# Taking a decay factor from a float32 exponential by DMA from chunk 8 on instead of chunk 12, in a fused linear-attention and feed-forward kernel

## The chip, the cores and the metric

The kernel runs on one core of a Trainium2 chip. The metric is the device time of one execution in microseconds (us). A core has a matrix engine (TensorE, PE in the profile, with its weight loads as PEld), a vector engine (VectorE, DVE), a scalar engine (ScalarE, ACT), a third elementwise engine (GpSimd, POOL) and SyncE (SP), which here issues all DMAs. Each engine works through its own list of instructions in order and waits on semaphores for the others.

## The reference, cut to what matters

The inputs are `q`, `k`, `v` and `alpha`, each of 4 batches x 8 heads x 768 positions x 48 (alpha between 0.8 and 1), and two weight matrices. First a gated linear attention:

```
state = alpha[t][:, None] * state + outer(k[t], v[t])    # 48 x 48 per batch and head
y[t]  = q[t] @ state
```

Then the heads are put side by side (3072 tokens x 384) and go through a feed-forward layer: `h = x @ w_in` (384 to 2048), `g = max(h, 0) ** 2`, `out = g @ w_out` (2048 to 384). All is float32 outside; the kernel computes its matmuls in bfloat16.

## The kernel before, in words

**Chunks.** The 3072 tokens are 24 chunks of 128 positions, 6 to a batch, and the recurrence is rewritten for chunks. With L = log(alpha) and the prefix sum of L inside the chunk, A = exp(prefix sum) and Ai = exp(-prefix sum) are factors per position, and qA = q * A, kI = k * Ai. Inside a chunk y is the masked score matrix (qA times kI transposed, positions up to the own one) times v; what came before adds qA times the running state. At the end of a chunk the state becomes (state + kI transposed times v) * ae, where ae = exp(sum of L over the whole chunk), one number for each of the 48 key dimensions of each head. So ae is equal to the last row (position 127) of A. The first four chunks are done as two pairs by another function (`add_super`, lines 593 to 775); chunks 4 to 23 by `add_chunk`, `add_scores` and `add_back`.

**The steps of a chunk** and their lines:

- four loads of 192 KB (alpha, q, k, v), issued by SP (line 349), up to six chunks ahead, in tiles that hold two chunks; the next user of a tile waits for the readers of the one before
- the logarithm of alpha into `L_s` on ScalarE (line 407), the cast of v to bfloat16 on GpSimd (line 412)
- `e_p0`, on TensorE: the prefix sum, one matmul of 128x384 with the triangle `utri_b` (line 417); in chunks under `TURN` four more matmuls of one column each (`L_s` as the weights, `ones_col` as the moving operand, line 419), which leave the chunk's sum with the key dimensions on the partitions
- on ScalarE: A (`e_A`, line 435) and Ai (`e_Ai`, line 439). In chunks under `TURN`, A is bfloat16, and two small exponentials (lines 442 and 445) turn the sums into `ae_s`. From `TURN` on, A is float32 (the tile `Af`, in which the element order is permuted so that the four head pairs of one key dimension lie side by side), and SP moves its last row into `ae_s` with two DMAs of 48 partitions x 4 values (`e_aed`, line 452)
- on VectorE: `qA_s` (line 463, or 466 when A is float32) and `kI_s` (line 469); both are transposed on TensorE (line 258 through a helper) and copied out by VectorE (`qkT`, line 372)
- scores on TensorE for two chunks at once from chunk 8 on (`e_p2`, into the tile `sc` and two further banks), masked by VectorE (`sm`, line 530)
- `e_ps` (line 555): kI transposed times v is added to the state in PSUM; this operation waits for `kI_s`, the cast v, `ae_s` and the copy of the state of the chunk before. `e_stm` on VectorE (line 564) multiplies the state by ae, `e_sb` on ScalarE (line 569) copies it out in bfloat16 for the next chunk. The last chunk of a batch has none of these three, but its factor is still written
- the output `e_p3a`, `e_p3b`, a copy (`xn`, line 370), a transpose and a copy into `xT_big`

Feed-forward work runs in groups of one, two or four chunks: the first layer (`add_moe1`: matmuls of `xT_big` with `w_in_b`), relu on ScalarE (line 819), square on VectorE (line 827), the second layer (`add_moe2`: 16 matmuls of 128x384 a chunk), a copy out of PSUM (lines 889, 891) and a store issued by SP (lines 898, 901).

**Order.** Nothing of this order is left to the chip. Each operation is put into a plan with its engine, an assumed duration, its predecessors and a priority; `Plan.run` (lines 99 to 143) places all of them by these numbers and the instructions are then written out in that order, engine by engine. The assumed durations are constants in the code, among them those that depend on `TURN`: a load 1.05 or 0.97, the prefix sum 0.27 or 0.17, A 0.38 or 0.76, `qA_s` 0.47 or 0.78, and for the factor's DMAs 0.4 plus a latency `AE_LAT` of 4.0, during which the planner puts other work before `e_ps`. A gate lets the prefix sum of a chunk start only when the feed-forward work has come far enough. PSUM has eight banks; five are shared by all of these steps, and a step takes a bank when its reader has released it.

Of the kernel before, what the change touches and what calls it, by code (L numbers as in the profile page):

```python
# [146 lines left out]
def kernel(  # L147
# [86 lines left out]
    w_out_b = consts.tile([P, FT, d_model], BF16)  # L234

    NBUF = 4
    TURN = 12
    AE_LAT = 4.0
    L_s = big.tile([P, NBUF, H, DP], BF16)
    nc.gpsimd.memset(L_s[:, :, :, D:], 0.0)  # L240
# [13 lines left out]
    def mm(*a, **kw):  # L254
        pin(nc.tensor.matmul(*a, **kw))  # L255
# [23 lines left out]
    def add(eng, dur, emit, *deps, **kw):  # L279
        return plan.add(Op(eng, dur, emit, deps, **kw))  # L280
# [59 lines left out]
    def add_load(s, nm):  # L340
# [10 lines left out]
        if 2 * NS <= s < 2 * NS + LB and (k - LB // 2) < NS:  # L351
            prev = SUP[k - LB // 2]["use_" + nm]
        pace = C[s - LB + 1]["use_" + nm] if s >= TURN + 2 else None
        d["ld_" + nm] = add("DMA", LD if s < TURN else 0.97, ld, prev, pace, lat=2.4)

# [41 lines left out]
    def add_chunk(s):  # L397
# [17 lines left out]
        def e_p0():  # L415
            pm = d["pm"] = psum(p0, [P, 512], FP32)
            mm(pm[:, 0:HD], lhsT=utri_b[:, 0, :], rhs=L[:, :, 0:D], start=True, stop=True)
            for p in range(NP if s < TURN else 0):
                mm(pm[:, HD + p:HD + p + 1], lhsT=L[:, 2 * p:2 * p + 2, :], rhs=ones_col,
                   start=True, stop=True)  # L420
        p0 = Op("PE", 0.27 if s < TURN else 0.17, e_p0, [ln], takes=GLA_BANKS, lat=0.17, **g)
        p0.gla = s

        def split(x, s):
            if s < TURN:
                return x.rearrange("p (h d) -> p h d", h=H)
            return x.rearrange("p (n j d) -> p n j d", n=NP, j=2)

        def e_A():
            if s < TURN:  # L430
                d["A"] = work.tile([P, H, D], BF16, name="A")
            else:
                d["Af"] = work.tile([P, 2, D, NP], FP32, name="Af", bufs=2)
                d["A"] = d["Af"].rearrange("p j d n -> p n j d")
            pin(nc.scalar.activation(d["A"], split(d["pm"][:, 0:HD], s), AF.Exp))  # L435
# [566 lines left out]
```

## Time and profile before

| what | value |
|---|---|
| median of 3 runs | 186.08 us (185.95 to 186.28) |
| the profiled execution | 185.27 us, of which its span is 183.6 us |
| granted TensorE clock | 1.00 throughout |
| ScalarE, A in bfloat16 (line 435, 8 times) | 491 ns |
| ScalarE, A in float32 (line 435, 12 times) | 867 ns |
| ScalarE, lines 442 and 445 (8 times each) | 168 ns |
| VectorE, `qA_s` from A (line 463, 8 times) | 580 ns |
| VectorE, `qA_s` from Af (line 466, 12 times) | 859 ns |
| SP, loads of chunks 4 to 23 (80 of 192 KB) | 3.6 to 3.7 us to landing |
| SP, `ae_s` from Af (line 452, 24 of 0.8 KB) | 2.0 us to landing |

How to read it: the span runs from the first to the last instruction of the profiled execution, and the time of the execution is a little longer. A row of a group gives the engine, the line, what is written and read, how often, and the mean duration; a line can be that of a helper (255 and 258 for TensorE's matmuls and transposes). The mean duration of a matmul includes its run through the engine; consecutive matmuls overlap, and what one costs is read from the distance of the starts. The chain is the work that ended last, followed back from its end; what is not on it ran beside it. "To landing" is from the issue on SP to the arrival of the data.

### The profile page before, as it was taken

The numbers are of one execution on the slowest core, as the hardware profiler recorded it, in microseconds if no ns is written. First come the engines' busy times: TensorE is split into PE (matmuls) and PEld (weight loads), VectorE is DVE, ScalarE is ACT, GpSimd is POOL, SyncE is SP. The second block draws the span as 40 slices with busy tenths as digits, with TensorE's granted clock in tenths as the row PEclk, the third lists the DMA queues.
The fourth block names the chain that finished last, engine by engine and source line by source line (L and its number), as shares of the span: only waits on it lengthen the run. The fifth ranks groups of instructions, "written<-read, shape, count | busy, mean of one in ns | idle before, by whom it ended". The sixth has DMA issues, their size and how long they took to land.

```text
span 183.6 us, 5043 instructions
## 1 busy us (share of the span) xinstructions
PE 177.2 (97%) x2000; PEld 133.5 (73%) x2000; DVE 135.0 (74%) x282; ACT 121.6 (66%) x257; POOL 30.5 (17%) x48
## 2 busy tenths in 40 slices
PE   7889899999999999999999999999999999999994
PEld 2567684666987877878867877777877878767863
DVE  6688779576998797776884997966996988852600
ACT  2567789357996994767739857847848768633721
POOL 6044667612111111111011011010010000000000
DMA  6999999899997989895999796877701101012012
GB/s 147 261 279 321 319 361 366 167 224 227 162 221 148 207 171 217 187 210 123 202 230 217 176 212 157 182 143 163 186 0 43 47 2 47 2 43 89 0 43 88
DMA packets 101256, 30.23 MB, mean 165 GB/s; under 512 B 93680, under 2 KB 100464, under 8 KB 101232
## 3 DMA queue, kind: packets, MB, share of 16 engines
q1 hardware_dynamic: 101232, 29.91, 70.2%
q8 instruction: 15, 0.25, 0.6%
q14 instruction: 9, 0.07, 0.1%
HBM read 25.17 MB, written 4.72 MB: 163 GB/s over the span
## 4 chain that ended last, share of the span: by engine, by line
PE 85%; ACT 5%; DMA 3%; DVE 3%; SPq 2%; issue 1%; ACTq 0%
PE bank L255 74%; PE bank L258 7%; DMA at<-in_alpha_dram 3%; PE sc L255 2%; PE st L255 2%; SPq L365 2%; ACT r L819 1%; DVE sm L530 1%; DVE qkT L372 1%; ACT raw L717 1%; ACT L_s L605 0%; DVE qA_s L653 0%; ACT w_in_b L308 0%; DVE st L747 0%; ACT L_s L407 0%
## 5 line engine op out<-in xcount | busy, mean ns | idle before, releaser
L255 PE MATMUL bank<-xT_big,w_in_b 128*128 128x256 bf16 (+2 forms) x600 | 73.3, 268 | 0.0
L255 PE MATMUL bank<-w_out_b,gT 128*128 128x384 bf16 (+2 forms) x400 | 71.9, 319 | 0.0
L819 ACT ACTIVATE r<-bank 128x512 bf16<-128x512 f32 x96 | 56.2, 603 | 15.6 <-PE bank L255 13.6
L255 PEld LDWEIGHTS <-w_in_b 128*128 128x128 bf16 x600 | 53.1, 98 | 9.4
L827 DVE TENSOR_TENSOR gT<-r 128x512 bf16<-128x512 bf16 x96 | 43.9, 480 | 11.5 <-ACT r L819 10.8
L255 PEld LDWEIGHTS <-gT 128*128 128x128 bf16 x400 | 36.3, 98 | 17.6
L412 POOL CAST vb<-vt 128x384 bf16<-128x384 f32 x20 | 11.0, 552 | 91.2 <-PE bank L255 56.7
L372 DVE COPY qkT<-bank 128x1024 bf16<-128x1024 bf16 (+1 forms) x26 | 16.4, 645 | 3.6 <-PE bank L258 3.4
L891 ACT COPY ob<-bank 128x384 f32<-128x384 f32 x17 | 8.2, 480 | 13.9 <-PE bank L255 13.7
L370 ACT CAST xn<-bank 128x384 bf16<-128x384 f32 x24 | 11.3, 483 | 9.0 <-PE bank L255 8.8
L530 DVE TENSOR_TENSOR sm<-sc,utri_b 128x512 bf16<-128x512 f32 x24 | 15.4, 683 | 2.0 <-PE sc L255 1.9
L372 DVE COPY xT_big<-bank 128x384 bf16<-128x384 bf16 x21 | 7.4, 354 | 10.8 <-PE bank L258 10.8
L255 PEld LDWEIGHTS <-qkT 64*128 64x128 bf16 (+2 forms) x304 | 10.5, 97 | 5.4 <-issue 2.2
L466 DVE TENSOR_TENSOR qA_s<-qt,Af 128x384 bf16<-128x384 f32 x12 | 10.3, 859 | 2.7 <-ACT Af L435 2.7
L407 ACT ACTIVATE L_s<-at 128x384 bf16<-128x384 f32 x20 | 10.4, 525 | 2.5 <-DMA at<-in_alpha_dram 2.5
L435 ACT ACTIVATE Af<-bank 128x384 f32<-128x384 f32 x12 | 10.4, 867 | 1.6 <-ACT xn L370 1.0
L469 DVE TENSOR_TENSOR kI_s<-kt,Ainv 128x384 bf16<-128x384 f32 x20 | 11.0, 552 | 0.0
L569 ACT CAST sb<-st 128x384 bf16<-128x384 f32 x16 | 7.7, 482 | 4.4 <-DVE st L564 4.3
L439 ACT ACTIVATE Ainv<-bank 128x384 bf16<-128x384 f32 x20 | 10.3, 513 | 0.0
L530 DVE TENSOR_TENSOR sm<-bank,utri_b 128x512 bf16<-128x512 f32 x16 | 10.2, 680 | 0.0
L255 PE MATMUL bank<-warm 128*128 128x256 bf16 (+2 forms) x36 | 8.1, 357 | 1.9 <-DVE both L218 1.1
L258 PE MATMUL bank<-ident_bf,qA_s 128*128 128x128 bf16 x96 | 9.3, 219 | 0.5 <-DVE qA_s L653 0.3
(73 smaller groups left out, 177.3 us busy)
## 6 DMA issues: line engine op xcount, KB each, us to landing
at<-in_alpha_dram SPq DMA_DIRECT2D x20, 192.0 KB, 3.6
qt<-in_q_dram SPq DMA_DIRECT2D x20, 192.0 KB, 3.7
kt<-in_k_dram SPq DMA_DIRECT2D x20, 192.0 KB, 3.7
vt<-in_v_dram SPq DMA_DIRECT2D x20, 192.0 KB, 3.7
out_dram<-ob SPq DMA_DIRECT2D x19, 192.0 KB, 2.7
wo<-in_moe_w_out_dram SPq DMA_DIRECT2D x4, 768.0 KB, 7.4
wi<-in_moe_w_in_dram SPq DMA_DIRECT2D x4, 384.0 KB, 7.2
wi<-in_moe_w_in_dram SPq DMA_DIRECT2D x2, 768.0 KB, 5.7
```

Of the source, the lines that this page charges most:

```text
L255: pin(nc.tensor.matmul(*a, **kw))
L258: pin(nc.tensor.transpose(*a))
L370: pin(nc.scalar.copy(out_t, in_t))
L372: pin(nc.vector.tensor_copy(out_t, in_t))
L407: pin(nc.scalar.activation(L[:, :, 0:D], d["at"], AF.Ln))
L412: pin(nc.gpsimd.tensor_copy(d["vb"], d["vt"]))
L435: pin(nc.scalar.activation(d["A"], split(d["pm"][:, 0:HD], s), AF.Exp))
L439: pin(nc.scalar.activation(d["Ai"], d["pm"][:, 0:HD].rearrange("p (h d) -> p h d", h=H), AF.Exp, scale=-1.0))
L469: pin(nc.vector.tensor_mul(kI[:, :, 0:D], d["kt"], d["Ai"]))
L530: pin(nc.vector.tensor_mul(d["sm"][:, hh], d["sc"][hh], utri_b.to_broadcast([P, NP, P])))
L819: pin(nc.scalar.activation(box["r"][:, 0:w], box["ph"][:, 0:w], AF.Relu))
L827: pin(nc.vector.tensor_mul(gT[g][:, f0:f0 + per, lo * P:lo * P + n], r, r))
```

## The change

`TURN` goes from 12 to 8. Chunks 8, 9, 10 and 11 now take their decay factor as chunks 12 to 23 do: their prefix sum has no `ones_col` matmuls, A is written as `Af` in float32, the two small exponentials are gone, `qA_s` is computed from `Af`, and two DMAs bring the factor into `ae_s`. The planner's constants for these four chunks change with it, and so does the pace that it assumes for the loads of chunks 10 to 13 (line 353), so that it places the work of these and the following chunks in another order. Up to the prefix sum of chunk 8 the order of TensorE's instructions is the one before.

```
     NBUF = 4
-    TURN = 12
+    TURN = 8
     AE_LAT = 4.0
```

The lines that read it:

```
pace = C[s - LB + 1]["use_" + nm] if s >= TURN + 2 else None
d["ld_" + nm] = add("DMA", LD if s < TURN else 0.97, ld, prev, pace, lat=2.4)
...
for p in range(NP if s < TURN else 0):
...
a_ = add("ACT", 0.38 if s < TURN else 0.76, e_A, p0, **g)
...
if s < TURN:
    ae0 = add("ACT", 0.18, e_ae0, p0, after(ai), **g)
    p0.gives = ae1 = add("ACT", 0.19, e_ae1, p0, after(ae0), **g)
else:
    p0.gives = ai
    ae1 = add("SPD", 0.4, e_aed, a_, lat=AE_LAT, **g)
    ae1.hold = 0.5
```

In SP's list the new pairs of DMAs stand: chunk 8's between the loads of chunk 9 and those of chunk 10; chunk 9's between those of chunk 10 and those of chunk 11; chunk 10's after the alpha and q loads of chunk 13; chunk 11's after the alpha load of chunk 14.

## The prediction

> **What bounds the kernel now.** I read the engine totals first, then the chain that ended last, then the busy times by stage, and last the places where the changed instructions stand. The totals and the chain by line of the page of before:
>
> ```profile
> span 183.6 us, 5043 instructions
> PE 177.2 (97%) x2000; PEld 133.5 (73%) x2000; DVE 135.0 (74%) x282; ACT 121.6 (66%) x257; POOL 30.5 (17%) x48
> PE 85%; ACT 5%; DMA 3%; DVE 3%; SPq 2%; issue 1%; ACTq 0%
> ```
>
> TensorE is busy for 97% and carries 85% of the chain. A pipelined busy time can hide waits, so I also read the chain in order of time (start, length, what). This stretch is the only one after 24 us in which the chain leaves TensorE for long:
>
> ```profile
> 58.27 0.66 PE bank L255 x4
> 58.95 0.26 ACT ob L891
> ...
> 61.24 0.17 ACT ae_s L445
> ...
> 63.82 1.89 DVE sm L530 x3
> 65.76 2.47 PE bank L255 x37
> ...
> 166.43 14.39 PE bank L255 x120
> 180.85 0.27 ACT ob L855
> ```
>
> From 58.95 to 65.76 us the chain runs through ScalarE and VectorE, but TensorE is not idle for it: in this stretch the timeline shows one real hole, where the last matmul of one group starts at 65.43 us and the next at 65.76, 0.33 where this form (three 128x256 matmuls in 0.33 us elsewhere in the chain) takes 0.11: 0.22 us lost. From 65.76 to 180.85 nothing but TensorE is on the chain. So after 24 us the time is the sum of what TensorE issues, plus whatever holds it.
>
> The stages (busy us per engine, granted clock, DMA share, GB/s), with the change inside the second and third:
>
> ```profile
> 54.00:66.00 12.00, 11.94 (x153) 9.67 (x151) 10.18 (x22) 9.63 (x25) 1.01 (x2) 1.00 0.88 172
> 66.00:82.00 16.00, 16.00 (x192) 12.37 (x189) 12.78 (x29) 10.85 (x26) 2.32 (x4) 1.00 1.00 205
> 82.00:166.00 84.00, 84.00 (x912) 64.85 (x910) 66.39 (x135) 57.40 (x113) 4.70 (x9) 1.00 0.53 123
> ```
>
> VectorE has 1.8 us free of 12, then 3.2 of 16. The DMA engines, at 0.53 where the present factor DMAs run, are full where the new ones go.
>
> **The change part by part.** For chunks 8 to 11 each:
>
> (1) TensorE drops the four `ones_col` matmuls of 128x1. The price is read from starts of neighbours in the timeline, first chunk 9, then chunk 12:
>
> ```profile
> 58.76 0.33 PE L255 MATMUL bank<-L_s,utri_b 128*128 128x384 bf16 x1
> 58.92 0.24 PE L255 MATMUL bank<-ones_col,L_s 128*128 128x1 bf16 x4
> 59.02 0.38 PE L255 MATMUL bank<-xT_big,w_in_b 128*128 128x256 bf16 x2
> ...
> 81.73 0.33 PE L255 MATMUL bank<-L_s,utri_b 128*128 128x384 bf16 x1
> 81.89 0.49 PE L255 MATMUL bank<-w_out_b,gT 128*128 128x384 bf16 x2
> ```
>
> With them the next matmul starts 59.02 - 58.76 = 0.26 us after the prefix-sum matmul, without them 81.89 - 81.73 = 0.16: 0.10 to 0.105 per chunk, 4 x 0.105 = 0.42 us, all on the path. The weight loads of these four (96 ns mean of the 48 loads from `L_s`) would be 16 x 0.096 = 1.5 us if they stood on the path; 0.105 for four of them says that they hide under the 128x384 matmul. The Trainium skill, "TensorE: Matmul & The Clock Gate", section "LDWEIGHTS (loading the stationary operand)", gives a load as its columns over 1.2, 107 ns for 128, an estimated 16 x 0.107 = 1.7 us if it bound here; by that rule the sum would be -1.7 instead of -0.42, and the trace speaks against it.
>
> (2) ScalarE: the first exponential writes float32 in a strided layout (Af, 867 ns mean of 12) instead of bfloat16 (A, 491 ns), +0.376; the two exponentials into `ae_s` (0.168 each, 0.336) go. Sum +0.04 per chunk, +0.16 in all. VectorE: `qA_s` from Af takes 859 ns, from A 580: +0.28, +1.1 us in all. Neither engine sets the pace in the present Af stage (57.4 and 66.4 of 84 us), so I cost them at nothing. What hides them is the matmuls in between; if that cover is gone the +1.1 is the upper bound, and below it is zero, since both engines gain work.
>
> (3) SP and DMA: per chunk two transfers of 0.8 KB, eight in all, in the same queue as the loads. The rows:
>
> ```profile
> L452 SPq DMA_DIRECT2D ae_s<-Af x24: 501/583/1281, 83.0 to 156.8; - x24
> DMA to landing us min/median/max: 1.6/2.0/3.3
> ```
>
> Two issues take about 1.2 us of SP (0.58 each). In the new order the pair of chunk 8 stands between the loads of chunks 9 and 10, that of chunk 9 between those of 10 and 11, that of chunk 10 behind the alpha and q loads of chunk 13, and that of chunk 11 behind alpha of chunk 14 (nothing reads that one, chunk 11 closes a batch). So every load behind them goes out up to 1.2 us later per pair, less where SP was held by a full queue anyway (at chunk 9's v load for 2.63 us, at chunk 12's alpha load for 2.02). The loads that ScalarE needs soonest are alpha of 11, 12 and 13: the 11th was issued at 59.22, the group of them landed in 3.4 to 4.4 us (median 3.8), and its logarithm started at 64.98. That leaves about 2 us for it. For 12 and 13 (issued 63.35 and 67.72, logarithms at 68.84 and 73.03) it leaves 1.7 and 1.5 before their two pairs' delay of at most 2.4. A logarithm that is 0.5 us late holds the relu behind it on ScalarE, and so a bank of TensorE. I take nothing, with 0 to 0.5 us as bounds.
>
> (4) The new wait: the state matmul (`e_ps`, line 560) now waits for the landing. TensorE runs in a fixed order, so everything behind it would wait too. The planner moves the state matmuls of chunks 8, 9 and 10 back behind other matmuls, so I compare times. State matmul of chunk 8: from the prefix-sum matmul of chunk 8 at 54.22, the new order has two prefix-sum matmuls (0.32), 9 first-layer matmuls of 128 columns (0.50), 16 of 384 columns (2.60), 11 transposes (0.61), the output group (0.37) and 15 of 256 columns (1.65): 6.05, so it stands at 60.3. In the same way chunk 9's stands at about 64.5 and chunk 10's at about 75.0. Landings: Af of chunk 8 would be ready at 54.73 + 0.87 = 55.6, SP is free at 55.66, the second issue starts at about 56.3 and lands at 58.3 (median) to 59.6 (longest). Chunk 9: second issue at about 61.0, landing 63.0 to 64.3. Chunk 10: second issue between 70.7 and 72.6, landing 72.7 to 75.9. At the median all three are in time, by 2.0, 1.5 and 0.4 to 2.3 us. I cost this wait at nothing, as the rows of this very transfer lie nearest. Its other end: a load at this place took up to 4.9 us (v, issues from 49.7 to 70.5); with that the lateness would be 0.9, 1.4 and up to 2.5 us, and since an earlier hold moves the later ones back, 2.5 us in all.
>
> The 0.22 us hole at 65.43 waits for VectorE's mask of the scores, behind a square that came late. The new order has another square there, so it may close; I count 0 to 0.22 as gain and take 0.
>
> Sum on the profiled execution: 183.6 - 0.42 = 183.2 us of span. That execution took 185.27, so 1.67 lies around its span; 184.85. It was 0.81 under the median of the runs shown, 186.08. Carried over: 186.08 - 0.42 = 185.66.
>
> **The rivals.**
>
> A. A late factor. As in (4): one landing that passes the 4.0 us that chunk 8 has, or the 3.5 that chunk 9 has, holds TensorE. For it: DMA share 0.88 to 1.00 here against 0.53 in the later stage, and the loads' 3.4 to 4.9 us. Against it: the small transfer has 0.8 KB where a load has 192, and 3.3 us was the longest of 24. It decides from 0.42 us of lateness on, that is 4.4 us for chunk 8 or 3.9 for chunk 9. One miss of 0.9: 186.08 - 0.42 + 0.9 = 186.6; all of it: 188.2. The Trainium skill, "DMA: Bandwidth & Descriptors", section "Anatomy of one DMA — SWDGE (gpsimd) path", puts a constant of about 2.0 us on every DMA; by that figure no landing is late and the sum stays at -0.42. The trace's 1.6 to 3.3 us is not constant, and the rows decide.
>
> B. VectorE becomes the bound. It is 85% busy from 54 to 66 us, and the chain already ran through it. All of (2) on the path: 186.08 - 0.42 + 1.1 + 0.16 = 186.9. Against it: from 82 us on the same forms run with TensorE at 84.0 of 84.0.
>
> C. The gain is eaten in part: a late logarithm or mask holds a bank for 0.2 to 0.4 us. 185.9.
>
> D. The 16 dropped weight loads were on the path after all, at 0.096 each: 186.08 - 1.5 = 184.6. Only the difference of the two starts in (1) speaks for or against it, and it is against.
>
> **How the numbers follow.** Forecast (185.66) 0.50; C 0.20; A 0.21; B 0.07; D 0.02. About 0.2%, 0.37 us, is what a measurement of this kernel can tell from no change. Faster: forecast and D, 0.52. Within: C, 0.20. Slower: A and B, 0.28. The range goes from 185.2 (the forecast less the hole of 0.22 and the runs' scatter of 0.2) to 187.0 (over B and a single miss in A); outside lie D and the worse half of A. The likeliest case by itself: 185.2 to 185.8.
>
> **What the changed profile would show.** (1) 16 `ones_col` matmuls instead of 32, and 0.16 us from prefix sum to next matmul at chunks 8 to 11. (2) 16 instructions each of Af and of `qA_s` from Af, 4 left in each `ae_s` line of ScalarE. (3) 32 issues at line 452, the first at about 56 us. (4) The state matmuls of chunks 8, 9, 10 at about 60.3, 64.5 and 75.0 with no hole before them. What would make me wrong: a hole before one of these with the `ae_s` DMA as its releaser (A), chain pieces of line 466 and 530 with holes after them (B), or a logarithm at line 407 that waits for its DMA (C).

## The result

The changed kernel is slower. Its median is 187.49 us (185.53 to 188.24, 18 runs) against 185.87 us (185.30 to 187.51, 18 runs) for the kernel before on the same chip: a ratio of 1.0082, with a 95% interval of 1.006 to 1.0103. The forecast was 185.66, with a range up to 187.0; both missed, and on the wrong side of no change. The profiled execution took 186.64 us with a span of 184.9, 1.3 more than the 183.6 before; it is one of the quicker ones of its kernel, so it shows most of the loss but not all of it.

### The profile page after: what moved, and what is told of

Read it like the earlier page. It is cut to its first block, busy times and chain, and to the rows that moved or that the text cites. A ratio compares the mean times of both kernels' runs of the same rounds, so it can differ in the third digit from the quotient of the medians.

```text
span 184.9 us, 5017 instructions
## 1 busy us (share of the span) xinstructions
PE 177.8 (96%) x1983; PEld 133.0 (72%) x1984; DVE 137.1 (74%) x284; ACT 121.2 (66%) x247; POOL 29.9 (16%) x48
## 4 chain that ended last, share of the span: by engine, by line
PE 80%; DMA 5%; ACT 5%; SPq 4%; DVE 3%; issue 1%; ACTq 0%
PE bank L255 69%; PE bank L258 7%; DMA at<-in_alpha_dram 5%; SPq L349 2%; PE sc L255 2%; SPq L365 2%; PE st L255 2%; ACT r L819 1%; DVE sm L530 1%; DVE qkT L372 1%; ACT Af L435 1%; ACT raw L717 1%; DVE qA_s L466 0%; ACT L_s L605 0%; DVE qA_s L653 0%
## 5 line engine op out<-in xcount | busy, mean ns | idle before, releaser
L891 ACT COPY ob<-bank 128x384 f32<-128x384 f32 x15 | 7.3, 484 | 15.9 <-PE bank L255 15.8
L466 DVE TENSOR_TENSOR qA_s<-qt,Af 128x384 bf16<-128x384 f32 x16 | 13.7, 859 | 5.3 <-ACT Af L435 5.3
L435 ACT ACTIVATE Af<-bank 128x384 f32<-128x384 f32 x16 | 13.9, 866 | 1.7 <-ACT xn L370 1.0
L564 DVE TENSOR_TENSOR st<-st,ae_s 128x384 f32<-128x384 f32 x16 | 9.0, 560 | 2.1 <-PE bank L255 1.3
```

What stands on the lines that cost most here:

```text
L466: pin(nc.vector.tensor_mul(qA[:, :, 0:D].rearrange(v4, j=2), d["qt"].rearrange(v4, j=2), d["A"]))
```

## The profile after

The totals and the chain by engine on the page of the changed kernel:

```profile
span 184.9 us, 5017 instructions
...
PE 177.8 (96%) x1983; PEld 133.0 (72%) x1984; DVE 137.1 (74%) x284; ACT 121.2 (66%) x247; POOL 29.9 (16%) x48
...
PE 80%; DMA 5%; ACT 5%; SPq 4%; DVE 3%; issue 1%; ACTq 0%
```

TensorE's share of the chain fell from 85 to 80%; SP's queue doubled to 4% and DMA rose from 3 to 5%. After 24 us the chain, in order of time (start, length, what), now leaves TensorE for long at two places:

```profile
60.81 0.58 SPq L452
61.40 0.05 issue
61.45 0.58 SPq L349
...
63.34 2.58 SPq L349
...
65.96 3.40 DMA at<-in_alpha_dram
...
69.81 0.85 ACT Af L435
...
70.68 0.87 DVE qA_s L466
...
105.92 1.10 ACT r L819 x2
...
107.04 0.42 DVE gT L827
107.46 1.81 DVE sm L530 x3
...
109.32 1.55 PE bank L255 x28
```

The first place runs, after some work of ScalarE, through one of the new factor issues (line 452). Behind it stand the four loads of a chunk, behind them the alpha load of the next (issued at 65.96), and behind its landing the logarithm and the exponential on ScalarE and `qA_s` on VectorE. The second place, at 106 us, lies 30 us behind the four chunks that were changed. By stage (busy us per engine, granted clock, DMA share, GB/s):

```profile
54.00:66.00 12.00, 12.00 (x141) 9.62 (x136) 10.63 (x23) 9.01 (x19) 1.49 (x3) 1.00 0.79 153
66.00:82.00 16.00, 15.89 (x163) 11.60 (x161) 13.16 (x28) 10.32 (x20) 1.54 (x3) 1.00 0.88 175
...
100.00:124.00 24.00, 23.23 (x254) 17.64 (x252) 19.88 (x40) 15.47 (x30) 1.82 (x3) 1.00 0.84 181
```

From 54 to 82 us the DMA engines moved less than before (153 and 175 GB/s against 172 and 205) although they had more to do. So the loss is not a want of DMA engines; the loads are issued late. And TensorE, at 24.00 of 24.00 from 100 to 124 us before, lost 0.77 us there.

Two rows of the groups say who waits. The last part of a row is the idle time of the engine ahead of the group, and what ended it. First before, then after:

```profile
L407 ACT ACTIVATE L_s<-at 128x384 bf16<-128x384 f32 x20 | 10.4, 525 | 2.5 <-DMA at<-in_alpha_dram 2.5
L564 DVE TENSOR_TENSOR st<-st,ae_s 128x384 f32<-128x384 f32 x16 | 8.9, 556 | 0.0
```

```profile
L407 ACT ACTIVATE L_s<-at 128x384 bf16<-128x384 f32 x20 | 10.3, 528 | 6.1 <-DMA at<-in_alpha_dram 6.1
L564 DVE TENSOR_TENSOR st<-st,ae_s 128x384 f32<-128x384 f32 x16 | 9.0, 560 | 2.1 <-PE bank L255 1.3 <-PE bank L258 0.8
```

ScalarE waits 3.6 us more for alpha: the logarithms of chunks 11, 12 and 13 waited 1.49, 0.79 and 1.00 us, where before none of them waited more than 0.03. VectorE, which before never waited ahead of the state multiply (`e_stm`, line 564), now waits 2.1 us. The row names TensorE as the releaser, but TensorE was long done. VectorE's timeline around the multiply of chunk 14, before and after (start, length, then the instruction):

```profile
102.88 1.09 DVE L827 TENSOR_TENSOR gT<-r 128x512 bf16<-128x512 bf16 x3
103.88 0.56 DVE L564 TENSOR_TENSOR st<-st,ae_s 128x384 f32<-128x384 f32 x1
104.35 0.68 DVE L372 COPY qkT<-bank 128x1024 bf16<-128x1024 bf16 x1
```

```profile
103.27 0.55 DVE L469 TENSOR_TENSOR kI_s<-kt,Ainv 128x384 bf16<-128x384 f32 x1
104.94 0.57 DVE L564 TENSOR_TENSOR st<-st,ae_s 128x384 f32<-128x384 f32 x1 [1.12 <-PE bank L255]
105.41 0.42 DVE L827 TENSOR_TENSOR gT<-r 128x512 bf16<-128x512 bf16 x1
105.75 0.68 DVE L372 COPY qkT<-bank 128x1024 bf16<-128x1024 bf16 x1
```

The state matmuls of chunk 14 (`e_ps`) had run from 102.85 on, without waiting for the factor: only the multiply reads `ae_s`. The second factor transfer landed at 104.82, and the multiply began 0.12 us later, as it did at the other two late chunks (90.41 and 90.54; 119.01 and 119.13). So it waited for the factor. Behind it in VectorE's list stand a square and the copy `qkT`, and TensorE waits for that copy, then for the masks:

```profile
106.49 0.40 PE L255 MATMUL bank<-qkT 64*128 64x128 bf16 x8 [0.57 <-DVE qkT L372]
...
109.32 0.33 PE L255 MATMUL bank<-sb,qkT 128*128 128x96 bf16 x4 [0.20 <-DVE sm L530]
```

Measured by the distance of the starts, these two holes are about 0.75 and 0.36 us. The waits at chunks 12 and 16 (0.21 and 0.78 us) left none of this size in this execution. The cause is seen in SP's list, before and after:

```profile
99.43 0.73 SPq L898 DMA_DIRECT2D out_dram<-ob  x1
100.22 0.42 SPq L349 DMA_DIRECT2D at<-in_alpha_dram  x1
100.74 1.29 SPq L452 DMA_DIRECT2D ae_s<-Af  x2
```

```profile
97.89 0.43 SPq L349 DMA_DIRECT2D at<-in_alpha_dram  x1
98.43 2.35 SPq L349 DMA_DIRECT2D qt<-in_q_dram  x1
100.87 1.20 SPq L349 DMA_DIRECT2D kt<-in_k_dram  x1
102.16 1.21 SPq L452 DMA_DIRECT2D ae_s<-Af  x2
```

`Af` of chunk 14 was ready at 97.81 (before: 98.70), yet its two factor DMAs were issued at 102.16 (before: 100.74), since SP was still busy with a q load of 2.35 us and a k load of 1.20. In the kernel before, this factor had landed at 103.61 and was used at 103.88: a slack of 0.27 us, the smallest of all.

## The experiments

Two theories stood against each other at first. By theory Q, the eight added issues make SP's list late, and with it later factors and alpha loads. By theory V, the float32 exponential and the strided `qA_s` cost ScalarE and VectorE time that is not hidden. A third, O, is that the planner's new order is worse by itself. Ratios are to the kernel before, run beside each kernel on the same chip: median 187.40 us beside the first four, 185.81 beside the next four, 185.70 beside the last four. The chip of the first four was slower, and more scattered, already with the kernel before.

**1. The float32 work without the DMAs.** Chunks 8 to 11 write `Af` and compute `qA_s` from it, but keep the `ones_col` matmuls and the small exponentials for the factor.

```diff
     TURN = 12
+    F32 = 8
...
         def e_A():
-            if s < TURN:
+            if s < F32:
...
         def e_qA():
-            if s < TURN:
+            if s < F32:
```

> Before, with only the float32 exponential and the multiply from it in chunks 8 to 11; the ones matmuls and the two small exponentials stay and there are no new DMAs. Theory Q (the eight new issues make SP's list and the loads late, so that later factors and alpha arrive late): within 0.3 us of before, and the state multiplies of chunks 12, 14 and 16 wait for nothing. Theory V (VectorE and ScalarE pay for the float32 form, up to 1.1 us): 0.6 to 1.3 us slower than before.

Measured: 187.26 us, ratio 1.0009 (0.9977 to 1.0041). Theory V asked for 0.6 to 1.3 us; the median is 0.14 faster. The interval, up to +0.77, does not rule out the lower end of that, but the profile shows no loss from the dearer work, as follows. The other half of the expectation missed: the multiply of chunk 14 waited 2.35 us for its factor, which SP issued at 103.29 (before: 100.74) though its list has no added entry. (The planner's durations of the two operations changed with the edit, and with them the order of some entries.) Behind this wait TensorE had holes of 1.67 and 0.36 us, about 2.0 together, and the span of this profile, 185.5, is 1.9 longer than that of before: the late factor makes up the whole difference. So the dearer work is hidden (theory V falls), and chunk 14 can be late without the new transfers too. Whether the kernel before was late there on this chip is not shown; no trace of it was kept beside these runs.

**2. The DMAs without the rest.** The kernel before, with two idle transfers of 48 partitions x 4 values for each of chunks 8 to 11 in the place where the change puts its factor DMAs; nobody reads them. The values are bfloat16, so each moves 0.4 KB instead of 0.8.

```diff
+        def e_idle():
+            for j in range(2):
+                pin(nc.sync.dma_start(out=idle_s[HF * j:HF * j + D, i, j], in_=...))
+        if 8 <= s < TURN:
+            add("SPD", 0.4, e_idle, a_, lat=AE_LAT, **g).hold = 0.5
```

> Before, with eight more small DMAs on SP at the place where the change has them, into a tile that nobody reads; the factors of chunks 8 to 11 still come from the two small exponentials. Theory Q: 0.8 to 2 us slower than before (186.7 to 187.9), with logarithms of chunks 11 to 13 and state multiplies of later chunks that wait for DMAs. Theory V, and theory O (the new order by itself costs the time): within 0.4 us of before.

Measured: 189.38 us, ratio 1.0097 (1.006 to 1.0134): the whole loss, with the computation of before. Its groups show the same two waits:

```profile
L408 ACT ACTIVATE L_s<-at 128x384 bf16<-128x384 f32 x20 | 10.4, 525 | 6.3 <-DMA at<-in_alpha_dram 6.3
L571 DVE TENSOR_TENSOR st<-st,ae_s 128x384 f32<-128x384 f32 x16 | 8.9, 556 | 2.3 <-DMA ae_s<-Af 1.3 <-PE bank L259 0.9
```

6.3 us for alpha (6.1 in the changed kernel) and 2.3 for the factor (2.1). Of the 6.3, 3.8 fall on chunks 4 and 5, before the idle transfers; the rest on the logarithms of chunks 11 (0.87) and 15 (1.61), where the changed kernel's stood at 11, 12 and 13. No engine's idle time is ended by one of the idle transfers; what costs is what they delay.

**3. The new order without the DMAs.** The plan is made with `TURN` = 8, but chunks 8 to 11 do the work of before, and their two small exponentials stand where the DMAs stood.

```diff
-    TURN = 12
+    TURN = 8
+    OPS = 12
...
-            for p in range(NP if s < TURN else 0):
+            for p in range(NP if s < OPS else 0):
...
         def e_aed():
+            if s < OPS:
+                e_ae0()
+                e_ae1()
+                return
```

> The changed kernel's plan, but chunks 8 to 11 emit the work of before: ones matmuls, bfloat16 exponential, the two small exponentials at the place in the order where the DMAs stood. Theory O: 1 us or more slower than before. Theories Q and V: within 0.4 us of before, since SP has no new issue and VectorE no dearer multiply.

Measured: 185.82 us, ratio 0.9921 (0.989 to 0.9952). The order is not to blame. Every factor was on time; that of chunk 14 landed at 104.17 for a multiply at 104.38. This is more than the "within 0.4 us" expected: on this chip the new order without the transfers is better than the old one. Why is not settled; a late factor at chunk 14 in the old order, as in experiment 1, would fit.

**4. Half of the change.** `TURN` = 10.

```diff
-    TURN = 12
+    TURN = 10
```

> The change for chunks 10 and 11 alone (TURN 10). Theory Q: between the two kernels, 0.3 to 1.0 us slower than before, since four issues are added instead of eight and they come after the loads of chunk 12. Theory V: half of the dearer multiplies less half of the matmuls, 0.2 to 0.4 us slower. If one late factor at chunk 14 makes the whole loss, it is either all there (1.2 us) or not at all.

Measured: 188.43 us, ratio 1.0049 (1.0015 to 1.0083): with half of the transfers, about half of the loss (though the intervals of this run and of experiment 2 overlap), and at the same place. The factor of chunk 10 was on time and that of chunk 14 was not: its multiply waited 2.44 us. Here the row names the releaser:

```profile
L564 DVE TENSOR_TENSOR st<-st,ae_s 128x384 f32<-128x384 f32 x16 | 8.9, 558 | 2.8 <-DMA ae_s<-Af 2.8
```

**5. The changed kernel again,** on the chip of the next runs.

```diff
-    TURN = 12
+    TURN = 8
```

> The changed kernel once more, beside the kernel before on one chip, as the yardstick for the runs beside it. Theory Q (late factors): 0.5 to 1.1% slower than before, and the sum of VectorE's idle time before the state multiplies of chunks 12, 14 and 16 makes 1 to 3 us.

Measured: 186.90 us, ratio 1.0074 (1.0035 to 1.0114). The multiplies of chunks 12, 14 and 16 waited 0.68, 0.92 and 0.74 us, all for `ae_s<-Af`; the loss and its places repeat.

**6. More time for the factor in the plan.** The changed kernel with a planned latency of 7.0 instead of 4.0.

```diff
-    TURN = 12
-    AE_LAT = 4.0
+    TURN = 8
+    AE_LAT = 7.0
```

> The changed kernel with AE_LAT 7.0 instead of 4.0: the planner leaves about 5 us more room (in its own numbers 3 us) between the exponential and the state multiply, the DMAs and their number stay. Theory Q: no idle time of VectorE before the state multiplies, and the kernel is 1 us or more faster than the changed one and 0.2 to 0.6 us faster than before, as the blind sum of 0.42 said. Theory L (the loss comes from late loads of alpha on ScalarE): as slow as the changed kernel within 0.4 us.

Measured: 186.60 us, ratio 1.004 (1.0014 to 1.0066). The gain of 1 us or more that theory Q expected is not there; perhaps half of the loss is gone, but the interval overlaps that of experiment 5. The factors of chunks 8 to 15 were on time. That of chunk 16 was issued at 117.35 and landed at 120.11, its multiply waited 2.34 us, and TensorE then had a hole of 1.98 us. The lateness moved; a larger constant in the plan does not make SP's list shorter.

**7. The issues on ScalarE.** All sixteen pairs of the changed kernel are issued by ScalarE.

```diff
-                pin(nc.sync.dma_start(out=ae_s[HF * j:HF * j + D, i, j], in_=d["Af"][P - 1:P, j]))
+                pin(nc.scalar.dma_start(out=ae_s[HF * j:HF * j + D, i, j], in_=d["Af"][P - 1:P, j]))
```

> The changed kernel with all 16 pairs of factor DMAs issued by ScalarE instead of SP; order otherwise the same. Theory Q: loads go out as in the kernel before, factors go out right behind their exponential, and no state multiply waits; the kernel is within 0.5 us of before or faster, unless the 32 issues cost ScalarE more than 0.3 us each, which shows as relus that come late. Theory L: logarithms of chunks 11 to 13 no longer wait, and the same gain comes from there.

Measured: 191.20 us, ratio 1.0301 (1.0265 to 1.0336). No factor was late, so the cause was gone, but a dearer one had taken its place. ScalarE's timeline at one pair:

```profile
89.14 0.54 ACT L439 ACTIVATE Ainv<-bank 128x384 bf16<-128x384 f32 x1
89.39 1.15 ACTq L452 DMA_DIRECT2D ae_s<-Af  x2
90.59 2.10 ACT L819 ACTIVATE r<-bank 128x512 bf16<-128x512 f32 x4 [0.91 <-PE bank L255]
```

The two issues hold ScalarE's list for 1.15 us, and it computes nothing for 0.91 of them. The row names TensorE as the releaser, but the relu starts 0.05 us after the issues end, and seven of the sixteen pairs are followed by just 0.91 us of idle time, whatever instruction comes next. The sixteen together left ScalarE idle for 15.1 us (0.80 to 1.39 each), and TensorE waits for the relus that come late: 2.3 us in five waits between 54 and 170 us, the longest 1.1.

**8. The kernel before with the larger latency,** to see what the constant does alone.

```diff
-    AE_LAT = 4.0
+    AE_LAT = 7.0
```

> The kernel before with AE_LAT 7.0. If the kernel before also loses to late factors in its slower executions (chunk 14 had 0.27 us to spare in its profile), this one is 0.3 to 1.2 us faster and scatters less. If it has no such loss, within 0.3 us.

Measured: 185.90 us, ratio 1.0012 (0.999 to 1.0035): nothing that can be told from no change. The larger constant alone brings nothing, so what experiment 6 may have gained belongs to the changed kernel's lateness.

**9. Only the four new pairs on GpSimd.** The changed kernel, in which the factor DMAs of chunks 8 to 11 alone are issued by GpSimd.

```diff
-                pin(nc.sync.dma_start(out=..., in_=d["Af"][P - 1:P, j]))
+                pin((nc.gpsimd if s < 12 else nc.sync).dma_start(out=..., in_=d["Af"][P - 1:P, j]))
```

> The changed kernel, order and work the same, with only the factor DMAs of chunks 8 to 11 issued by GpSimd; those of chunks 12 to 23 stay on SP. SP's list is then as free as with twelve pairs. Theory Q: the state multiplies of chunks 12, 14 and 16 wait for at most 0.3 us together and the kernel is 0.5 to 1.5 us faster than the changed one, 0 to 0.6 us faster than before. If the place of the later factors in the new order, and not the eight new issues, makes them late, it stays as slow as the changed kernel.

Measured: 184.94 us (184.69 to 185.04, 10 runs), ratio 0.9949 (0.9929 to 0.9968): faster than both kernels, against before by 0.76 us at the median where 0 to 0.6 had been expected, and with little scatter. The work, the order and the bytes are those of the changed kernel; only the engine that issues eight small transfers is another. Its two rows, and the issue of the factor of chunk 14 on SP:

```profile
L407 ACT ACTIVATE L_s<-at 128x384 bf16<-128x384 f32 x20 | 10.3, 524 | 2.8 <-DMA at<-in_alpha_dram 2.8
L564 DVE TENSOR_TENSOR st<-st,ae_s 128x384 f32<-128x384 f32 x16 | 8.9, 557 | 0.6 <-DMA ae_s<-Af 0.6
...
97.65 1.85 SPq L349 DMA_DIRECT2D kt<-in_k_dram  x1
99.60 1.43 SPq L452 DMA_DIRECT2D ae_s<-Af  x2
```

Both waits are back near those of before; the 0.6 us stand at chunk 16, where 0.3 at most had been expected. From 54 to 82 us the DMA engines now move 196 and 199 GB/s (changed kernel: 153 and 175), and TensorE is busy for the whole of 54 to 124 us. How far the delay travels is seen in the landings of alpha (us), of which the changed kernel and this one have the same plan:

| chunk | 11 | 12 | 13 | 14 | 15 | 16 | 17 | 18 | 19 |
|---|---|---|---|---|---|---|---|---|---|
| changed kernel | 66.07 | 69.36 | 72.87 | 78.46 | 83.42 | 90.01 | 96.66 | 103.03 | 107.98 |
| new pairs on GpSimd | 62.43 | 67.03 | 70.43 | 74.55 | 79.59 | 85.12 | 95.36 | 100.62 | 105.77 |

The alphas land 1.3 to 4.9 us later in the changed kernel from chunk 11 to chunk 19, long after the last added pair. From 55 to 104 us the issues in its SP list follow each other with pauses of at most 0.50 us, so it cannot catch up; without the eight issues, 4.6 us of SP at 0.58 each, the list had one pause of 2.1 us (at 82.5). The factor pairs of chunks 12, 14 and 16 stand in that list, and went out at 84.62, 99.60 and 114.64 here, against 86.62, 102.16 and 116.25.

The Trainium skill, "DMA: Bandwidth & Descriptors", section "Issuing engines are not separate DMA queues", says that transfers run on the same 16 DMA engines whoever starts them, and that issuing from several engines saves only the time of the issuing sequencer, usually small beside the transfer. The trace agrees that the transfer itself gained nothing: the pairs of chunks 8 to 10 took 3.6 to 4.1 us to land from GpSimd, 2.4 to 3.1 from SP. But in a list without slack the small time of the issues, 0.58 us each, goes with a difference of 1.3% (1.0074 against 0.9949, each against the kernel before on its own chip).

**10. All sixteen pairs on GpSimd.**

```diff
-                pin(nc.sync.dma_start(out=..., in_=d["Af"][P - 1:P, j]))
+                pin(nc.gpsimd.dma_start(out=..., in_=d["Af"][P - 1:P, j]))
```

> The changed kernel with all 16 pairs of factor DMAs on GpSimd. Theory Q: no late factor, unless one waits behind a cast of v that waits for its buffer; as fast as with the DMAs of chunks 8 to 11 alone on GpSimd, or faster by up to 0.5 us. A factor that stands behind a waiting cast would show as idle time of VectorE of 1 us or more.

Measured: 185.02 us, ratio 0.9965 (0.9949 to 0.9982). No state multiply waited:

```profile
L452 POOL DMA_DIRECT2D ae_s<-Af x32 | 16.1, 508 | 39.5 <-ACT Af L435 35.5 <-DVE sm L530 2.0 <-DVE xT_big L372 2.0
...
L564 DVE TENSOR_TENSOR st<-st,ae_s 128x384 f32<-128x384 f32 x16 | 8.9, 557 | 0.0
```

GpSimd sat idle for 39.5 us ahead of these issues, mostly until `Af` was ready; it has the room that SP lacks.

**11. The kernel before with its twelve pairs on GpSimd.** The same edit with `TURN` = 12.

```diff
-                pin(nc.sync.dma_start(out=..., in_=d["Af"][P - 1:P, j]))
+                pin(nc.gpsimd.dma_start(out=..., in_=d["Af"][P - 1:P, j]))
```

> The kernel before with its 12 pairs on GpSimd. Theory Q: where the kernel before has late factors in part of its executions, this one is 0.2 to 0.8 us faster at the median and scatters less; if SP was never late for it, within 0.2 us.

Measured: 185.51 us, ratio 0.999 (0.9967 to 1.0013). So the kernel before loses little by issuing on SP, and the gain in 9 and 10 is not merely GpSimd's. Beside experiment 10, this is the change with SP's list taken out of both sides: 185.02 - 185.51 = -0.49 us, with about 0.5 us either way by the two intervals, where step (1) of the prediction has -0.42. The profiled execution of this run, 186.74 us, is one of its two slowest. What it lost, it lost ahead of every factor: alpha of chunk 4 took 9.3 us to land (7.4 in the profile of before), and TensorE waited for its logarithm:

```profile
37.05 0.32 PE L255 MATMUL bank<-L_s,utri_b 128*128 128x384 bf16 x1 [1.03 <-ACT L_s L407]
```

**12. The changed kernel without the three unread pairs.** The factors of chunks 11, 17 and 23, which close a batch and which nobody reads, are not fetched.

```diff
-            ae1 = add("SPD", 0.4, e_aed, a_, lat=AE_LAT, **g)
-            ae1.hold = 0.5
+            ae1 = None
+            if not last:
+                ae1 = add("SPD", 0.4, e_aed, a_, lat=AE_LAT, **g)
+                ae1.hold = 0.5
```

> The changed kernel without the factor DMAs of chunks 11, 17 and 23, which nobody reads: 13 pairs on SP instead of 16, and the state multiplies see the same data. Theory Q: part of the loss goes, 0.3 to 1 us faster than the changed kernel, with chunk 14's wait shorter than 1 us, since chunk 11's pair stood behind alpha of chunk 14.

Measured: 186.75 us, ratio 1.0069 (1.0046 to 1.0093), no recovery that can be told from experiment 5. The expectation missed. With the pairs gone the plan came out in another order, and the pair of chunk 12 went out at 88.89 instead of 86.62; its multiply then waited 1.23 us, that of chunk 14 0.91:

```profile
L566 DVE TENSOR_TENSOR st<-st,ae_s 128x384 f32<-128x384 f32 x16 | 9.0, 560 | 2.5 <-DMA ae_s<-Af 2.5
```

In SP's list the pair of chunk 12 now stands behind alpha and q of chunk 16 (issued at 86.22 and 86.91, the latter for 1.88 us), where in the changed kernel it stood behind alpha alone (85.86). Nor was the list earlier: one k load held SP for 2.36 us at 75.72, and alpha of chunk 16 went out 0.36 us later than in the changed kernel. So the number of issues alone does not set the loss; the place of a pair behind loads, and how long SP is held at them, do too.

## Why the prediction was wrong

**What held.** Step (1): 16 `ones_col` matmuls are left, and the next matmul starts 0.16 or 0.17 us after the prefix sum at chunks 9 and 8 (58.54 - 58.38, 54.27 - 54.10). With SP's list out of the way the change is worth -0.49 us (experiments 10 and 11) with -0.42 worked out; the size agrees, but the interval reaches to about zero, so this is no proof of it. Step (2): 16 exponentials of 866 ns, 16 `qA_s` of 859, and experiment 1 shows no cost of them (ratio 1.0009). The state matmuls of chunks 8, 9 and 10 started at 60.2, 64.4 and 75.3, where 60.3, 64.5 and 75.0 had been worked out, and the factors of all three were on time. The hole of 0.22 us at 65.43, taken at nothing, did close.

**The step that failed is (4): "I cost this wait at nothing", together with (3): "I take nothing, with 0 to 0.5 us as bounds".** Three things were wrong in them.

- The engine. The prediction has the state matmul at line 560 wait for the landing, as the description of the steps also says, and weighed TensorE's times. That matmul is behind the factor only in the plan; on the chip the reader of `ae_s` is VectorE's multiply at line 564. A late factor holds VectorE's list (`qkT`, squares, masks), and TensorE through it.
- The chunks. Only the new consumers were priced, chunks 8 to 10. The late ones are 12, 14 and 16, whose DMAs are not new: they stand behind the new ones in SP's list. Chunk 14 had 0.27 us of slack, which the trace of before shows and the prediction did not weigh.
- The delay. Step (3) saw that "every load behind them goes out up to 1.2 us later per pair", but followed it to three alpha loads only and bounded the whole at 0.5 us. Even there its own numbers spoke against nothing: a delay of up to 2.4 us against slacks of 2.0, 1.7 and 1.5. The alphas landed 3.25, 1.72 and 1.31 us later than before, the logarithms waited 1.49, 0.79 and 1.00, and the delay did not fade for forty microseconds. (Alpha of chunk 11 was issued 2.23 us later, as the two pairs ahead of it would have it, and took 1.02 longer to land.)

**The account of the profiled execution.** The distances of TensorE's starts give +0.75 and +0.36 for the late factor of chunk 14; +0.24 at 71.25, where `qA_s` is late behind a late logarithm; four smaller ones of 0.10 to 0.19 between 73 and 97 us, 0.55 together, whose causes were not separated; +0.22 at 26.7, before the change acts, which the profile of before lacks and those of the experiments have too. Against them stand -0.42 and -0.22 (the hole at 65.43). The sum is +1.5, where the span grew by 1.3. Beside experiment 9, which has the same order, the account needs no such terms: its span is 183.3, 1.6 shorter, and the holes from 71 to 109 us, 1.9 together, are absent there, against one of 0.18 that it has alone.

**The rivals.** A, a late factor, had the right kind of mechanism and its 186.6 to 188.2 holds the result, but its condition (a landing over 4.4 us after the issue) never came: no factor took longer than 3.8 (4.1 in experiment 5). They were issued late. So its number is right by luck. The Trainium skill, "DMA: Bandwidth & Descriptors", section "Anatomy of one DMA — SWDGE (gpsimd) path", which A names, gives its 2.0 us for DMAs issued by GpSimd; these were issued by SP, and took 1.7 to 3.8 us. B's dearer work cost nothing that experiment 1 could show. C's sign is there, logarithms that wait for their DMA, and the hole of 0.24 us behind one lies within C's 0.2 to 0.4, though it is `qA_s` that TensorE waits for there and not a bank; it is the smaller part of the loss. D's -1.5 lies outside what experiments 10 and 11 leave.

**What stays open.** The changed kernel's executions scatter from 185.5 to 188.2 us, and those of experiment 9 only from 184.7 to 185.0. The lateness of SP's list goes with the scatter here, but it is not its only source: with every pair on GpSimd, experiment 11 still has two executions of 186.7 among twelve, one of them late from alpha of chunk 4 on. What makes one execution later than another is not shown. Nor is it shown how the 1.6 us of the medians split between late factors and late alphas. In the profiled execution the holes behind the factor are 1.1 us and that behind an alpha 0.24; in experiment 2's profile, two behind late alphas (0.89 at 67.03 and 0.94 at 86.69) outweigh the two behind the factor of chunk 14 (0.84 and 0.33). Whether the new transfers delay the list by their issue time alone, or also by their place in SP's DMA queue, was not separated; 4.6 us of issues against delays of up to 4.9 us leaves room for both.

## What to carry to other kernels

A transfer that is added to an in-order issuing list costs what it delays: go down the list behind it, to the end of the stretch in which the list has no pause, and hold each entry's slack (landing to use, in the trace of before) against the delay; the smallest slack, here 0.27 us, some 45 us behind the first added issue, made the largest loss of the profiled execution. Find the reader of the data by the operands of the instruction, not by the plan's dependencies. Where a list is full, a small transfer can go on the queue of an engine that idles there (GpSimd: -0.5%), but not on that of one that feeds the bound (ScalarE: +3.0%).

## What the runs showed of the hardware

- A DMA issue is not free for the issuing engine. On ScalarE a pair of 0.8 KB transfers cost 0.80 to 1.39 us of idle time, 0.91 at the median; on SP an issue of such a transfer took 0.58 us, and that of a load up to 3.4 us (the k load at 30.45 us of the kernel before).
- The small transfers that GpSimd issued for chunks 8 to 10 landed 3.6 to 4.1 us after the first issue (56.15 to 60.20, 60.52 to 64.09, 70.67 to 74.78); those that SP issued, 2.4 to 3.1 (55.48 to 57.88, 59.85 to 62.67, 71.53 to 74.63). The slower path gave the faster kernel. In the quiet stretch at the end it was GpSimd's that were quicker: the pairs of chunks 20, 21 and 23 took 2.0 to 2.1 us in experiment 10, 2.3 from SP in the kernel before. The Trainium skill, "DMA: Bandwidth & Descriptors", section "Latency and other measured facts", has the first byte at about 0.6 us for SP's path and 1 us for GpSimd's: the direction agrees for chunks 8 to 10, where the measured difference, to the landing of a pair, is 0.7 to 1.7 us, and not at the end.
- The profile can name an engine as the releaser of a wait that a DMA ended: the 1.12 us ahead of the multiply of chunk 14 stand under TensorE, while the landing 0.12 us before its start, and the same wait in experiments 4 and 5, say that it was the factor.
